# The end of attention and the gating of a fused attention and expert kernel: an own order for the last turn, a PSUM pool per bank, ten warm-up products instead of fourteen, and other queues for three loads of v and eighteen clears

## The chip, the cores and the metric

The kernel runs on one core of one Trainium2 chip. The time is device microseconds of one execution, as the median of the runs shown. The engines are TensorE (PE, with its weight loads as PEld), VectorE (DVE), ScalarE (ACT), GpSimd (POOL) and SyncE (SP). A queue of SP, ACT or POOL issues transfers to 16 DMA engines.

## The reference

Attention over 8 batches, 8 heads, 576 positions and 64 columns, with a causal mask over blocks of 64, then a layer of 8 experts in which each token goes to its best expert and an expert keeps its 80 tokens of the highest gate:

```python
scores = scale * np.matmul(q, k.transpose(0, 1, 3, 2))
scores = np.where(block_i >= block_j, scores, -1000000000.0)
attn = np.exp(scores - np.max(scores, axis=-1, keepdims=True))
attn = attn / (np.sum(attn, axis=-1, keepdims=True) + 1e-09)
x = np.matmul(attn, v)            # then (8, 8, 576, 64) -> (4608, 512)
logits = x @ w_gate
expert_idx = np.argmax(logits, axis=1)
probs = np.exp(logits - logits.max(-1, keepdims=True))
probs /= probs.sum(-1, keepdims=True) + 1e-09
gate_w = probs[np.arange(N), expert_idx]
for e in range(E):
    tok_idx = np.where(expert_idx == e)[0]
    if len(tok_idx) > capacity:
        tok_idx = tok_idx[np.argpartition(-gate_w[tok_idx], capacity)[:capacity]]
    h = np.maximum(x[tok_idx] @ w1[e], 0.0)
    out[tok_idx] = gate_w[tok_idx, None] * (h @ w2[e])
```

All tokens that no expert keeps have zeros in `out`, so at most 640 of 4608 rows carry a result and the rest must be cleared.

## The kernel before, in words

**Attention** goes by pairs of heads, 32 of them (4 in each of 8 batches, `NP = 4`). The program runs a loop over turns `i`, and in each turn a table `TURN` of (offset, operation) says what is issued for which pair: the loads five turns ahead, the transposes of q and k (DVE, L430) two turns ahead, the scores (PE, L459), the maxima (DVE, L476) and the exponentials (ACT, L487) of the pair after, and for the pair of the turn the transposes of the exponentials back (`back`, PE, L514, in four pieces A, B, C, L), the copies of these out of PSUM (`take`, ACT or DVE, L545, to `PT`), and the products with v (`values`, PE, L534). Two more copies, V0 and V1, put the result into `xT`; `flip` (DVE, L296) transposes it into `Y`, and `store` (SP, L300 to L303) writes `Y` and the reciprocal sums `rs` of a batch to `xs` in DRAM. PSUM has 8 banks, and a table gives each use its banks.

**Gating** comes once per batch of four pairs and is dealt out over later turns by the slots `pe`, `t` and `ta` of the table: `logits` (PE, L311, 8 products of 288 columns in two banks), two copies to `lgT` (ACT, L315), `logits2` (PE, L322, ten transposes), then on DVE `products` (L328), `shift`, `first_of` and `weight`, with `expo` on ACT between them, `turn` (L368, `sp`, on POOL for batches 0 to 6 and on DVE for batch 7), `turn2` (PE, L377) and `placed` (DVE, L383, to `Wt`). In the drain behind the last turn the rest of batch 6 goes first, then the whole chain of batch 7.

**The choice of tokens** follows: maxima of `Wt` (DVE, L705), `near` and `spread` (L714, L717), a ranking on PE (`ranked`, L727, into two PSUM tiles), counts on DVE and ACT (L772, L775), one-hot rows (L780), picks on PE (L788), and the list `gi` (L792). With it POOL issues eight gathers of 80 rows of `xs` (L802).

**The experts**: `divide` (DVE, L896) makes `xn` of gathered rows, `prepare` (L916) transposes it, `first` (PE, L907) and `second` (PE, L957) are the two products, and POOL scatters the results (L966). The weights are 16 matrices of 2 MB; three are loaded on POOL during attention, the others on SP (L256): one behind the last store of `xs`, two that wait for the first gather, and three that wait for the fourth.

**Warm-up products** (`warm`, L555) are matmuls of 128x512 whose result nothing reads. `WARM` gives their number for five places: 8 at the start of the program, 14 behind `logits2` of the last batch, 5 behind its `turn2`, 2 behind `ranked`, 12 behind the picks. The statement stands late in the program; `issue_after` names the instruction behind which the scheduler may put them.

**The queues**: `load_v` (L423, L425) issues three transfers per pair on POOL. `clear` (L163) writes 512 KB of zeros to `out`; 18 of them are needed. Nine are issued on POOL, one every third turn from turn 6, and the other nine on SP behind the stores of the last batch.

## Time and profile before

| what | value |
|---|---|
| median of three runs | 435.67 us (434.53 to 435.85) |
| the profiled execution | 436.88 us |
| its span, first to last instruction | 435.1 us |
| mean granted clock of TensorE | 0.95 |
| PE busy, share of the span | 389.9 us, 90% |
| ACT busy | 302.5 us, 70% |
| DVE busy | 276.1 us, 63% |
| POOL busy | 143.8 us, 33% |
| DMA moved | 84.31 MB, 194 GB/s over the span |

The profiled execution took 1.21 us more than the median of the runs, and its span is 1.78 us shorter than its own time. Attention fills the span up to about 298 us, the last gating and the choice of tokens the time up to about 322, and the experts the rest. A granted clock of 1.0 is 2.4 GHz, one of 0.5 is 1.2 GHz. A window's five engines are PE, PEld, DVE, ACT and POOL. In the rows of a timeline the first two numbers are the start and the length of a group of instructions in us; what stands in brackets is the idle time of the engine before it and the work that ended it.

### The profile page before, as it was taken

What the parts mean: (1) busy time and instruction counts of PE and PEld (TensorE: products, weight loads), DVE (VectorE), ACT (ScalarE), POOL (GpSimd) and SP (SyncE); (2) the same over time, 40 slices, a digit from 0 to 9 for tenths busy, and PEclk for the clock granted to TensorE, in tenths of its full rate; (3) what the DMA queues carried; (4) which work ended last, traced back from release to release, by engine and by line L of the source; (5) the groups of instructions that cost most, each with busy time, mean ns of one, the idle gap of its engine ahead of it and who ended that gap; (6) DMA issues with size and microseconds to landing.
All of it is one profiled execution on the core that took longest, in us unless ns stands there. A gap on an engine that the chain in (4) does not pass through costs nothing. (4 is left out here: it accounts for less than half of the span.)

```text
span 435.1 us, 13902 instructions
## 1 busy us (share of the span) xinstructions
PE 389.9 (90%) x5363; PEld 260.8 (60%) x5363; DVE 276.1 (63%) x768; ACT 302.5 (70%) x954; POOL 143.8 (33%) x273
## 2 busy tenths in 40 slices
PE   3799999999999999999999999985773999999960
PEld 2476666666766676676667666663553955555530
DVE  3568878998899799899898899873432130100010
ACT  0579999999999999999999999992020223333240
POOL 8523533454345335434454244200235001000010
PEclk9889999999999999999999999999666899999995
DMA  9999999899999999999899983140899999999000
GB/s 132 156 133 166 135 180 199 201 160 179 183 235 181 158 207 140 188 202 193 133 201 201 146 191 87 50 112 8 275 369 268 391 395 399 396 396 346 23 19 19
DMA packets 196071, 84.31 MB, mean 194 GB/s; under 512 B 160221, under 2 KB 178653, under 8 KB 196000
## 3 DMA queue, kind: packets, MB, share of 16 engines
q1 hardware_dynamic: 185424, 60.18, 64.0%
q0 software_dynamic: 8208, 22.89, 20.1%
q8 instruction: 44, 0.72, 0.8%
q10 hardware_dynamic: 2368, 0.30, 0.6%
q14 instruction: 27, 0.22, 0.2%
HBM read 63.21 MB, written 20.33 MB: 192 GB/s over the span
## 5 line engine op out<-in xcount | busy, mean ns | idle before, releaser
L487 ACT ACTIVATE P<-bank,negm 128x192 f32<-128x192 f32 (+2 forms) x320 | 162.2, 591 | 0.0
L459 PE MATMUL bank<-T,qt 64*128 64x320 f32 (+3 forms) x512 | 109.3, 516 | 7.8 <-POOL qt L437 4.1
L476 DVE TENSOR_REDUCE negm<-bank 128x1 f32<-128x192 f32 (+1 forms) x192 | 87.7, 472 | 27.2 <-PE bank L466 27.0
L545 ACT COPY PT<-bank 128x512 f32<-128x512 f32 x192 | 91.3, 584 | 8.3 <-PE bank L514 8.3
L534 PE MATMUL bank<-PT,vn 128*64 128x384 f32 (+5 forms) x768 | 93.8, 384 | 0.5 <-ACT PT L545 0.5
L487 ACT ACTIVATION_READ_ACCUMULATOR P<-bank,negm 128x1 f32 x320 | 89.6, 281 | 0.0
L514 PEld LDWEIGHTS bank<-ident,P 64*128 64x128 f32 x1664 | 66.0, 140 | 20.8 <-ACT PT L545 19.9
L437 POOL TENSOR_SCALAR qt<-T 128x512 f32<-128x512 f32 x64 | 28.0, 448 | 145.8 <-DVE raw L476 142.3
L514 PE MATMUL bank<-ident,P 64*128 64x64 f32 x1664 | 72.7, 227 | 1.3 <-ACT PT L545 0.7
L534 PEld LDWEIGHTS bank<-PT,vn 128*64 128x64 f32 x768 | 47.4, 137 | 40.6 <-issue 31.6
L459 PEld LDWEIGHTS bank<-T,qt 64*128 64x128 f32 x512 | 44.7, 191 | 23.1 <-issue 7.2
L423 POOL DMA_DIRECT2D vn<-in_v_dram x64 | 50.2, 786 | 0.3 <-issue 0.3
L476 DVE TENSOR_REDUCE raw<-bank 128x1 f32<-128x64 f32 (+1 forms) x128 | 48.5, 434 | 1.2 <-PE bank L459 1.2
L430 DVE STREAM_TRANSPOSE T<-ld 128x576 f32<-128x576 f32 x64 | 49.0, 767 | 0.2
L907 PEld LDWEIGHTS ps<-xsT,w 128*64 128x64 f32 x1024 | 38.5, 144 | 3.2 <-issue 1.9
L907 PE MATMUL ps<-xsT,w 128*64 128x80 f32 x1024 | 40.2, 241 | 0.0
L957 PE MATMUL av<-w,hT 128*32 128x512 f32 (+1 forms) x280 | 37.5, 594 | 0.0
L961 DVE SCALAR_TENSOR_TENSOR y<-av,comb,yt 80x512 f32<-80x512 f32 x7 | 5.2, 746 | 50.6 <-ACT yt L960 50.6
L966 POOL DMA_INDIRECT out_dram<-y,si x8 | 7.4, 924 | 82.3 <-DVE y L961 57.8
L456 PEld LDWEIGHTS bank<-T,qt 64*128 64x128 f32 x256 | 24.3, 196 | 12.0 <-issue 11.3
L957 PE MATMUL ps<-w,hT 128*32 128x512 f32 (+1 forms) x72 | 29.2, 548 | 0.0
L927 ACT ACTIVATE hT<-ps 128x320 f32<-128x320 f32 x16 | 7.0, 438 | 31.4 <-PE ps L907 31.4
(172 smaller groups left out, 399.0 us busy)
## 6 DMA issues: line engine op xcount, KB each, us to landing
w<-in_moe_w_dram SPq DMA_DIRECT2D x13, 2048.0 KB, 21.2
ld<-in_q_dram SPq DMA_DIRECT2D x128, 72.0 KB, 4.3
xs<-Y SPq DMA_DIRECT2D x32, 288.0 KB, 5.7
ld<-in_k_dram SPq DMA_DIRECT2D x124, 72.0 KB, 4.7
vn<-in_v_dram POOLq DMA_DIRECT2D x64, 128.0 KB, 4.4
out_dram<-zero POOLq DMA_DIRECT2D x9, 512.0 KB, 5.1
out_dram<-zero SPq DMA_DIRECT2D x9, 512.0 KB, 5.6
w<-in_moe_w_dram POOLq DMA_DIRECT2D x8, 512.0 KB, 6.7
```

Of the source, the lines that this page charges most:

```text
L423: nc.gpsimd.dma_start(self.vn[:, h], v[b, h0 + h, 0:512].rearrange("(j p) d -> p j d", p=P))
L430: nc.vector.transpose(t, self.nat[x].rearrange("p g d -> p (g d)"))
L437: nc.gpsimd.tensor_scalar(to, from_, scalar1=SCALE, scalar2=1.0, op0=ALU.mult, op1=ALU.mult)
L456: nc.tensor.matmul(s[h][:, c:c + n], lhsT=q_[:, b0:b0 + P], rhs=k_[:, k0:k0 + n], start=False, stop=False)
L459: nc.tensor.matmul(s[h][:, c:c + n], lhsT=q_[:, BLK + P * t:BLK + P * (t + 1)], rhs=k_[:, 0:n], start=(c == 0), stop=(g == "1"))
L476: nc.vector.tensor_reduce(to[:, b, h:h + 1], self.s[g][h][:, c:c + n], axis=AX.X, op=ALU.max, negate=True)
L487: nc.scalar.activation(Pt[self.i % 2][u][:, h, 0:n], self.s[g][h][:, c:c + n], AF.Exp, bias=self.negm[:, t, h:h + 1], scale=1.0, accum_out ...
L514: nc.tensor.transpose(pt[c][:, n_ * BLK:(n_ + 1) * BLK], row[u][r, h, P * j:P * (j + 1)], ident[r, r])
L534: nc.tensor.matmul(to, lhsT=self.vt[:, h, :] if j == 4 else self.vn[:, h, j, :], rhs=self.PT[:, h, row, b0:b1].rearrange("p b r -> p (b r) ...
L545: (nc.scalar.copy if TAKE[x] == "a" else nc.vector.tensor_copy)(*self.out.pop(x))
L907: yield nc.tensor.matmul(dst(b)[64 * c:64 * (c + 1)], lhsT=w_[:, a, col:col + 64], rhs=x_[:, a], start=(a == 0), stop=(a == n - 1))
L957: last = nc.tensor.matmul(to[col:col + s1 - s0, c0:c1], lhsT=hT[:, a, s0:s1], rhs=w_[:, a, c0:c1], start=(a == ends[0]), stop=(a == ends[1 ...
```

## The change

1. The last turn has a table of its own, `LAST`, with its own banks (`LAST_BANKS`): the pieces B, A, C and L go to banks 4 and 5, 0 and 1, 6 and 7, and 2, and `values` to bank 3. The copies of the pieces are split between ACT and DVE by name.
2. The loop ends with turn 31 and not two turns later. What followed in the two empty turns and the drain is written out: V0 of the last pair is copied half by ACT and half by DVE, the logits of the last batch are issued ahead of the last two flips, the second copy to `lgT` goes to DVE, `turn2` of batch 6 comes behind `logits2` of batch 7 in bank 3, and `turn2` of batch 7 goes to bank 2.
3. PSUM has one pool per bank instead of one pool with eight tiles, and behind attention the pool `ps_m2` is made second instead of last, so that the uses behind attention fall on other banks.
4. Fourteen warm-up products behind `logits2` become ten, behind `turn2` of batch 6.
5. `load_v` of pairs 0, 1 and 2 goes to SP.
6. The eighteen clears are all on POOL: four at the start of each of the turns 27 to 30, and two at the start of turn 31.

```diff
-WARM = [8, 14, 5, 2, 12]
+WARM = [8, 10, 5, 2, 12]
...
+LAST_BANKS = {"B": (4, 5), "A": (0, 1), "C": (6, 7), "L": (2,), "av": (3,)}
+LAST = (
+    (0, "pe"),
+    (0, "back", "B"),
+    (-1, "take", "V1", "v"),
+    (0, "soft", "34", 1),
+    (-1, "take", "V0", "v"),
+    (0, "back", "A"),
+    (0, "take", "B0", "v"),
+    (0, "take", "B1", "a"),
+    (0, "t"),
...
+    (0, "back", "C"),
+    (0, "take", "A1", "a"),
+    (0, "take", "A0", "v"),
+    (0, "back", "L"),
+    (0, "take", "C0", "a"),
+    (0, "take", "C1", "v"),
+    (0, "take", "L", "a"),
+    (0, "values"),
+    (0, "t"),
...
+    (0, "ta"),
+    (0, "t"),
...
-    psp = attp.enter_context(tc.tile_pool(name="psp", bufs=1, space=PSUM))
+    psp = [attp.enter_context(tc.tile_pool(name=f"psp{i}", bufs=1, space=PSUM)) for i in range(8)]
...
+        def logits_out(self, lt):
             for c in range(2):
-                nc.scalar.copy(lgT[:, BLK + 288 * c:BLK + 288 * (c + 1)], lt[c][:, 0:288])
+                copy = nc.vector.tensor_copy if c and self.b == B - 1 else nc.scalar.copy
+                copy(lgT[:, BLK + 288 * c:BLK + 288 * (c + 1)], lt[c][:, 0:288])
...
         def load_v(self):
+            eng = nc.sync if self.i < 3 else nc.gpsimd
...
-        for i in range(-LEAD, n + 2):
+        for i in range(-LEAD, n):
...
-            if i >= 4 and i % 3 == 0 and i < n:
+            for _ in range(4 if i >= n - 5 else 0):
                 clear(cleared)
                 cleared += 1
...
-        while pe_ or small or acts:
-            pe()
-            for _ in range(8):
-                t()
-            ta()
-            if turns:
-                bt, mark = turns.pop(0)
-                bt.turn2(banks("g")[0])
-                mark()
         bt = batches[B - 1]
         for _ in bt.recip():
             pass
+        to, from_ = pairs[n - 1].out.pop("V0")
+        half = to.shape[1] // 2
+        pairs[n - 1].take("V1", "v")
+        nc.scalar.copy(to[:, 0:half], from_[:, 0:half])
+        nc.vector.tensor_copy(to[:, half:], from_[:, half:])
+        lt = bt.logits_of()
+        for p_ in pairs[n - 2:]:
+            p_.flip()
         bt.store()
-        bt.logits()
+        bt.logits_out(lt)
+        ta()
+        while not turns:
+            t()
         bt.logits2()
+        bt_, mark = turns.pop(0)
+        bt_.turn2(banks("av")[0])
+        mark()
         for _ in (*bt.products(), *bt.shift()):
             pass
         bt.expo()
+        while small:
+            t()
         for _ in (*bt.first_of(), *bt.weight()):
             pass
         bt.turn(nc.vector, 2)
-        bt.turn2(banks("g")[0])
+        bt.turn2(banks("L")[0])
...
     ps_s = ctx.enter_context(tc.tile_pool(name="ps_s", bufs=2, **ps))
+    ps_m = ctx.enter_context(tc.tile_pool(name="ps_m2", bufs=3, **ps))
     ps_s4 = ctx.enter_context(tc.tile_pool(name="ps_s4", bufs=1, **ps))
     ps_a = ctx.enter_context(tc.tile_pool(name="ps_a", bufs=1, **ps))
-    ps_m = ctx.enter_context(tc.tile_pool(name="ps_m2", bufs=3, **ps))
...
-    for k, ins in enumerate((bt.turned, bt.last, ranked, picked)):
+    for k, ins in enumerate((bt_.last, bt.last, ranked, picked)):
         warm(WARM[1 + k], wt[:, k % 2], ins)
```

On PE, from the end of attention to the ranking, the kernel before has this order; `bank` with `sp` is `turn2`, `bank` with `xT` the logits, `bank` with `lgT` the ten transposes of `logits2`, and `ps` with `identr` the warm-up products:

```order
L377 MATMUL bank_5528<-sp,sameR_110 32x40 [waits Pool_49]
L311 MATMUL bank_5549<-xT,wgd 32x288 [waits DVE_49]
...
L322 MATMUL bank_5561<-ident,lgT 128x64 [waits Activation_49]
...
L377 MATMUL bank_5596<-sp,sameR_110 32x40 [waits DVE_49,PE_49]
...
L555 MATMUL ps_5774<-identr 128x512 x19
L727 MATMUL ps<-spread,before_117 128x96 [waits DVE_49,PE_49]
```

And the changed kernel this one:

```order
L345 MATMUL bank_5555<-xT,wgd 32x288 [waits DVE_49]
...
L360 MATMUL bank_5581<-ident,lgT 128x64 [waits Activation_49]
L360 MATMUL bank_5582<-ident,lgT 128x64 [waits DVE_49]
...
L415 MATMUL bank_5593<-sp,sameR_110 32x40 [waits Pool_49]
L415 MATMUL bank_5593<-sp,sameR_110 32x40 x7
L595 MATMUL ps_5801<-identr 128x512 x10
L415 MATMUL bank_5626<-sp,sameR_110 32x40 [waits DVE_49]
...
L595 MATMUL ps_5801<-identr 128x512 x5
L774 MATMUL ps<-spread,before_117 128x96 [waits DVE_49,PE_49]
```

`turn2` of batch 6 has moved from ahead of the logits to behind `logits2`; before, all nineteen warm-up products stand behind `turn2` of batch 7 and ahead of the ranking, and now ten of them stand ahead of that `turn2` and five behind it.

On SP, behind the stores of the last batch, the kernel before has these rows, `zero` being the clears and `w` the weights of the experts:

```order
L303 DMA xs<-Y 32x18x128 x4
L163 DMA out_dram<-zero 128x1024 x9
L256 DMA w<-in_moe_w_dram 128x4x1024
L256 DMA w<-in_moe_w_dram 128x8x512
L256 DMA w<-in_moe_w_dram 128x4x1024
L256 DMA w<-in_moe_w_dram 128x8x512
```

And the changed kernel these:

```order
L335 DMA xs<-Y 32x18x128 x4
L288 DMA w<-in_moe_w_dram 128x4x1024
L288 DMA w<-in_moe_w_dram 128x8x512
L288 DMA w<-in_moe_w_dram 128x4x1024 x2
L288 DMA w<-in_moe_w_dram 128x8x512
```

The nine clears are gone from between the last store and the first of these weights, and two weights of the kind 128x4x1024 (`w1`) now follow each other, the second of them ahead of a `w2`.

On POOL, at the start of the program, the kernel before issues v of pair 0 between the clearing of `wgd` and the first constants:

```order
L569 MEMSET wgd 128x128
L423 DMA vn<-in_v_dram 128x4x64 x2
L425 DMA vt_139<-in_v_dram 64x2x64
L198 MEMSET dl 128x45
L199 MEMSET zero 128x1024
```

In the changed kernel the constants follow at once:

```order
L609 MEMSET wgd 128x128
L230 MEMSET dl 128x45
L231 MEMSET zero 128x1024
```

Three issues of transfers have left POOL ahead of its constants.

## Rows read from the trace of the kernel before

**Rows 1.** Windows: from:to, length, busy us (instructions) of five engines, clock, DMA share, GB/s.

```profile
270.00:280.00 10.00, 9.97 (x140) 6.57 (x136) 9.13 (x24) 10.00 (x38) 3.44 (x7) 1.00 0.22 81
300.00:310.00 10.00, 5.13 (x63) 3.43 (x64) 6.52 (x31) 1.03 (x3) 1.23 (x4) 0.62 0.49 109
360.00:370.00 10.00, 10.00 (x180) 5.90 (x176) 0.75 (x1) 2.92 (x5) 0.92 (x1) 1.00 1.03 400
19.00:26.00 7.00, 6.31 (x64) 5.49 (x66) 3.00 (x7) 4.73 (x19) 0.00 (x0) 0.51 1.03 134
```

**Rows 2.** Timeline of the start: issues on ACT and POOL, first work of DVE.

```profile
0.78 2.12 ACTq L415 DMA_DIRECT2D ld<-in_k_dram  x4
3.03 1.78 POOL L423 DMA_DIRECT2D vn<-in_v_dram  x2
4.76 0.67 POOL L425 DMA_DIRECT2D vt<-in_v_dram  x1
...
9.20 0.17 DVE L226 TENSOR_TENSOR iota_c<-sameR,iota_c 128x16 f32<-128x16 f32 x1 [1.69 <-POOL iota_c L224]
...
9.59 1.44 DVE L430 STREAM_TRANSPOSE T<-ld 128x576 f32<-128x576 f32 x2
```

**Rows 3.** DMA issues of 1.2 to 2.5 us: count, KB each, us to landing.

```profile
ld<-in_k_dram ACTq DMA_DIRECT2D x4, 72.0 KB, 4.0
```

**Rows 4.** Timeline of the last turn and the last gating.

```profile
291.03 1.97 PE L514 MATMUL bank<-ident,P 64*128 64x64 f32 x48 [0.57 <-DVE prod L328]
...
294.70 2.70 PE L534 MATMUL bank<-PT,vn 128*64 128x384 f32 x20 [0.52 <-ACT PT L545]
...
299.67 0.79 POOL L368 TENSOR_TENSOR sp<-Gm,sameE 128x320 f32<-128x320 f32 x1 [21.77 <-DVE Gm L360]
...
301.21 1.18 PE L311 MATMUL bank<-xT,wgd 128*32 128x288 f32 x16 [0.35 <-DVE Wt L383]
...
303.69 0.68 DVE L328 TENSOR_TENSOR prod<-bank,rs 128x80 f32<-128x80 f32 x4 [1.51 <-PE bank L322]
```

**Rows 5.** Timeline of the ranking: warm-up products and what stands around them.

```profile
307.55 0.50 PE L377 MATMUL bank<-sp,sameR 128*32 128x40 f32 x16 [3.80 <-DVE sp L368]
307.99 6.77 PE L555 MATMUL ps<-identr 128*128 128x512 f32 x19
...
309.22 0.61 DVE L717 TENSOR_TENSOR spread<-near,sameR 128x192 f32<-128x192 f32 x2
...
314.60 0.58 PE L727 MATMUL ps<-spread,before 128*128 128x96 f32 x4
```

**Rows 6.** Timeline from the clears on SP to the first expert.

```profile
307.37 11.72 SPq L163 DMA_DIRECT2D out_dram<-zero  x9
...
321.76 1.11 POOL L802 DMA_INDIRECT xg<-xs,gi  x1 [9.21 <-ACT occ L849]
...
331.41 0.81 DVE L896 TENSOR_TENSOR xn<-xg 80x256 f32<-80x256 f32 x2 [10.53 <-DMA xg<-xs,gi]
```

**Rows 7.** DMA issues, whole program, then of 319 to 320, then of 416 to 424.

```profile
xg<-xs,gi POOLq DMA_INDIRECT x8, 9.9
...
w<-in_moe_w_dram SPq DMA_DIRECT2D x1, 2048.0 KB, 16.9
...
out_dram<-y,si POOLq DMA_INDIRECT x2, 2.9
```

**Rows 8.** Timeline of PE in the first two experts.

```profile
334.92 7.05 PE L907 MATMUL ps<-xsT,w 128*64 128x80 f32 x128
...
342.32 4.65 PE L907 MATMUL ps<-xsT,w 128*64 128x80 f32 x128
```

**Rows 9.** The clears on POOL: ns min/median/max, first and last start, us to landing.

```profile
L163 POOL DMA_DIRECT2D out_dram<-zero x9: 584/584/612, 71.0 to 277.0; - x9
...
DMA to landing us min/median/max: 4.6/5.3/6.4
```

**Rows 10.** Timeline of POOL in one turn late in attention.

```profile
267.94 0.88 POOL L437 TENSOR_SCALAR qt<-T 128x512 f32<-128x512 f32 x2 [4.98 <-DVE raw L476]
```

More of the change, by code (lines that the diff above doesn't have):

```diff
@@ L91 @@
     (3, "load_v"),
+)
+LAST_BANKS = {"B": (4, 5), "A": (0, 1), "C": (6, 7), "L": (2,), "av": (3,)}
[11 more added lines that the diff above has]
+    (0, "t"),
+    (0, "t"),
+    (0, "back", "C"),
[6 more added lines that the diff above has]
+    (0, "values"),
+    (0, "t"),
+    (0, "t"),
+    (0, "t"),
+    (0, "t"),
+    (0, "ta"),
+    (0, "t"),
+    (0, "t"),
+    (0, "t"),
 )
@@ L271, in tile_attn_moe, with banks @@
     attp = ExitStack()
-    psp = attp.enter_context(tc.tile_pool(name="psp", bufs=1, space=PSUM))
-    def banks(use):
-        return [psp.tile([P, 512], F32, name=f"bank{i}") for i in BANKS[use]]
+    psp = [attp.enter_context(tc.tile_pool(name=f"psp{i}", bufs=1, space=PSUM)) for i in range(8)]
+    def banks(use, where=BANKS):
+        return [psp[i].tile([P, 512], F32, name=f"bank{i}") for i in where[use]]
     class Batch:
@@ L306, in logits, with logits_of @@
         def logits(self):
+            self.logits_out(self.logits_of())
+        def logits_of(self):
             lt = banks("g")
@@ L313, in logits @@
                                      tile_position=(0, 32 * pr))
+            return lt
+        def logits_out(self, lt):
             for c in range(2):
-                nc.scalar.copy(lgT[:, BLK + 288 * c:BLK + 288 * (c + 1)], lt[c][:, 0:288])
+                copy = nc.vector.tensor_copy if c and self.b == B - 1 else nc.scalar.copy
+                copy(lgT[:, BLK + 288 * c:BLK + 288 * (c + 1)], lt[c][:, 0:288])
         def logits2(self):
@@ L403, in __init__ @@
             self.out = {}
+            self.where = LAST_BANKS if i == n - 1 else BANKS
             self.T = {}
@@ L420, in load_v @@
             b, h0 = self.b, self.h0
+            eng = nc.sync if self.i < 3 else nc.gpsimd
             self.vn = ld.tile([P, 2, 4, D], F32, name="vn", bufs=4)
             for h in range(2):
-                nc.gpsimd.dma_start(self.vn[:, h], v[b, h0 + h, 0:512].rearrange("(j p) d -> p j d", p=P))
+                eng.dma_start(self.vn[:, h], v[b, h0 + h, 0:512].rearrange("(j p) d -> p j d", p=P))
             self.vt = VT[self.i % 4]
-            nc.gpsimd.dma_start(self.vt[0:BLK], v[b, h0:h0 + 2, 512:576].rearrange("h p d -> p h d"))
+            eng.dma_start(self.vt[0:BLK], v[b, h0:h0 + 2, 512:576].rearrange("h p d -> p h d"))
         def prep(self, x):
@@ L498, in back @@
                 self.PT = big.tile([P, 2, 4, 8, BLK], F32, name="PT")
-            pt = banks(x)
+            pt = banks(x, self.where)
             halves = [slice(c * BLK, (c + 1) * BLK) for c in range(2)]
@@ L522, in values @@
         def values(self):
-            (av,), a0 = banks("av"), self.last[:, 4 * BLK:5 * BLK]
+            (av,), a0 = banks("av", self.where), self.last[:, 4 * BLK:5 * BLK]
             if turns:
@@ L541, in flip, with take @@
             self.bt.flip(self.pr)
-        def take(self, x):
-            (nc.scalar.copy if TAKE[x] == "a" else nc.vector.tensor_copy)(*self.out.pop(x))
+        def take(self, x, eng=None):
+            (nc.scalar.copy if (eng or TAKE[x]) == "a" else nc.vector.tensor_copy)(*self.out.pop(x))
     def warm(n, wt, after=None):
@@ L633, in tile_attn_moe @@
                 next(early, None)
-            for d, what, *args in TURN:
+            for d, what, *args in TURN if i < n - 1 else LAST:
                 if what in slots_:
                     slots_[what]()
-                elif 0 <= i + d < n and not (what == "flip" and i + d >= n - NP):
+                elif 0 <= i + d < n and not (what == "flip" and n - NP <= i + d < n - 2):
                     getattr(pairs[i + d], what)(*args)
-            if n - NP <= i + valued < n:
+            if n - NP <= i + valued < n - 2:
                 pairs[i + valued].flip()
```

## The prediction, before the run

> **What bounds the kernel now.** I read the windows first, since each stage has its own limit. Late in attention ACT is busy for 10.00 of 10 us and PE for 9.97: nothing but less work or an earlier start helps there. In the experts PE is busy for 10.00 of 10 while the weights arrive at 400 GB/s. Between the two, from 300 to 310, PE has work for 5.13 us, DVE for 6.52, ACT for 1.03 and POOL for 1.23 [rows 1]: a chain of single steps, and every microsecond taken out of it is a microsecond of the end. So I then read the timeline of that chain [rows 4 to 6], and the start, where the first work is a chain too [rows 2, 3]. A measurement of this kernel can tell about 0.3% (1.3 us) from no change.
>
> **Part 1, v of three pairs on SP.** DVE's first transpose T starts at 9.59, right behind the product with iota_c at 9.20, which waited for POOL. POOL's constants wait in line behind three issues for v, from 3.03 to 5.43 [rows 2]. Without these 2.4 us the constants end 2.4 us earlier and T could start at 7.2. Its data are there: k of pair 0 is issued on ACT from 0.78 to 2.90, and lands 4.0 later, at 6.9 [rows 2, 3]. I take a gain of **2.3**; the bounds are 0 (q or k lands just before 9.59) and 2.4. On SP the nine issues stand behind the loads of pairs 2, 3 and 4. What they push back there is pair 3 and later, wanted a turn (8.25 us, the distance of POOL's two issues for successive pairs) or more after the start: no cost, and if that cover fails, nine issues of about 0.53 (k: 2.12 for four) are 4.8 us on SP, of which the spare turn takes all.
>
> **Part 2, the last turn and the last gating.** Before, the 48 transposes at 291.03 waited 0.57 for DVE's `prod` in banks that they share, and `values` came at 294.70. With banks of its own the last turn has no such wait; with V0 moved from ACT, which copies the pieces, to DVE, I take 0.6, so `values` runs from 294.1 to 296.8 and, with half a copy of V0 on each engine and two flips of some 0.8, DVE is done at 299.3. The logits don't wait for the flips, and their second copy goes to DVE: the ten transposes can follow at 299.75, and DVE's products at 300.5. Before, the rest of batch 6 stood in between: its `sp` on POOL at 299.67, then turn2 and placed, so that the logits began at 301.21 and the products at 303.69 [rows 4]. That is 3.2 earlier. What is late next is batch 6 itself: its `sp` still comes at about 300.4 to 301.2, but now only its own turn2 waits for it.
>
> **Part 3, the warm-up products and the ranking.** `spread` was done at 309.83, yet the ranking started at 314.60: PE was running nineteen warm-up products from 307.99 to 314.76 (6.77, 0.356 each) [rows 5]. These 4.8 us lay on the path. Now ten of them run behind turn2 of batch 6, from about 301.6: 3.6 us, to 305.2. From products to `spread` is 309.83 - 303.69 = 6.14, and turn2 of batch 7 comes 3.86 into it, at 307.55 [rows 5]. So turn2 could start at 304.35 and has to wait to 305.2, 0.85 more; behind it `spread` takes 2.28 to 307.5, which the five remaining products (1.8) just fit. The ranking starts at 307.7 instead of 314.6: **6.9**, part 2 included. Bounds: no wait, 7.8. At the clock of 0.62 in that window [rows 1] a product took 0.356, so at 0.5 it takes 0.44, the ten end at 306.0 and the wait is 1.7; with the flips 0.3 late the low end is 5.8.
>
> **Part 4, pools.** One pool per bank lets a use wait for its own bank only: in no row but the 0.57 of part 2 does it matter. In the new order of the ranking the tile that ACT counts from is finished one group later: I take 0.3 off, between 0 and 0.45 (a group of 0.58 overlaps the next). **-0.3.**
>
> **Part 5, the clears.** Nine clears on SP took 11.72 us to issue from 307.37, ahead of a weight of 2 MB that landed 16.9 after its issue at 319.5. So the first gather, at 321.76, met a full set of queues: its `xn` came at 331.41, 9.65 later [rows 6, 7]; the eight gathers' median is 9.9, and the last two scatters, of the same size of rows in empty queues, took 2.9 [rows 7]. Now the stores end near 303.6, only that one weight follows (at 400 GB/s [rows 1] 5.2 us, with the stores ahead of it some 8: landed near 312), and the gather comes at about 315. From both sides: 2.9 as in empty queues, 9.65 as now. Being issued into queues that are empty but for its seven followers it is nearer the 2.9; I take 4.5, a gain of **5.15** (0 to 6.75). The Trainium skill, "DMA: Bandwidth & Descriptors", section "Anatomy of one DMA — SWDGE (gpsimd) path", gives about 2.0 us and the bytes over 436 GB/s for a transfer that GpSimd issues: an estimate of 2.4 us for 80 rows of 2080 bytes, by which the sum would be 2.1 us less, 417.5.
>
> Their new place costs nothing as long as POOL has room: it waits 4.98 of each turn for DVE [rows 10], four issues of 0.584 to 0.612 [rows 9] need 2.4, and the DMA share from 270 to 280 is 0.22 [rows 1], as no loads of q and k are left. The cover ends at 4.98/4 = 1.25 per issue; the nearest dearer row is SP's, 11.72/9 = 1.30, by which five turns would lose 0.2 each, 1 us. Before, the nine issues on POOL fell into turns in which DVE was busy (9.13 of 10 in 270 to 280), and the longest took 0.612. The Trainium skill, "SBUF — State Buffer", section "A bandwidth-pool intuition that's wrong (but worth ruling out)", says that a transfer issued by GpSimd that takes some 620 ns alone takes some 3100 beside a VectorE copy; four of those would need 12.4 us a turn, 7.4 more than is free, and the sum would be some 33 us worse. The trace disagrees so far, with 0.612 as its longest; I give that rule 1 chance in 100, among those of slower.
>
> **Part 6, the first expert.** From the first `xn` at 331.41 to the full row of the second expert at 342.32 are 10.9 us. In them 128 products take 7.05, which take 4.65 in the row behind [rows 8]: PE came out of its wait for the gather at the lower clock. With that wait shorter (twelve warm-up products, 4.3 us, nearly fill 4.5) most of the 2.4 comes back. I take **2.0**; bounds 0 (the low clock stays) and 3.2 (2.4, and the second divide of 0.81 [rows 6], which the first products no longer stand behind). The fourth `w1` now goes ahead of a `w2` on SP and waits for the first expert's products to end: that `w2` then lands some 7 us ahead of its use. No cost, and no gain, since PE is full from there on [rows 1].
>
> **Sum.** 2.3 + 6.9 - 0.3 + 5.15 + 2.0 = 16.05. The profiled execution would go from 436.88 to 420.8; it stands 1.21 above the median, so the median goes from 435.67 to **419.6**. All bounds at their best give 20.15 (415.5), all at their worst 5.35 (430.3).
>
> **Rivals.**
> - *The gathers stay slow* (15%). If what fills the queues at 322 is the weights and not the clears, 9.65 stays and part 5 gives 0: 424.8. For it: the weight landed 16.9 after its issue, so it flowed right through the gathers. Against: it waited behind 4.7 MB of clears.
> - *The start is held by loads* (10%). If q of pair 0 lands only at 9.5, part 1 gives nothing: 421.9.
> - *The start gains more* (8%). From 19 to 26 the clock is 0.51 and PE has 6.31 busy us of 7 [rows 1]. If the earlier v or the shifted constants close the idle time ahead of it, half of 6.31 comes back, 3.1: 416.5.
> - *POOL's queue blocks* (4%, slower). In the order of POOL each transfer waits for the one eight places back. With three loads of v and four clears a turn, that one was issued 8/7 of a turn before, 9.4 us. A clear lands 4.6 to 6.4 after its issue [rows 9]: nothing waits. But if the landing stretches to the 16.9 of the weight [rows 7], each turn becomes 16.9 x 7/8 = 14.8 instead of 8.25, and qt of the next pair, behind the clears on POOL, is that late: four turns of 6.5, 26 us, 445.7. It decides at a landing of 9.4; for it speaks only that clears will now follow each other at 0.6, against it the DMA share of 0.22.
> - *Nothing shows* (1%): part 2 and 3 are given back whole in a later wait, and the gathers too.
>
> **How the numbers follow.** The forecast as summed has 61%, the named rivals the rest, and 1% is for other mishaps. The first three rivals and the bounds of the forecast's own terms lie between 414 and 426, where I leave out the all-worst sum and the slower case: that holds some 8 in 10. Faster by over 0.3%: 0.95; within: 0.01; slower: 0.04.
>
> **What would show it.** T on DVE near 7.2; products of batch 7 some 3 us earlier against the end of the last `soft` and the ranking right behind `spread`, with ten warm-up products ending by 306 less the start's gain; clears on POOL of 0.6, with POOL's qt no later in its turn; SP's weight right behind the stores; the first `xg` landing in under 6 us; the first expert's 128 products at under 6 us. The forecast is wrong if turns 27 to 31 are longer than 8.25, if the landing of the clears exceeds 9.4, or if `xn` still waits 9 us behind the first gather.

## The result, and the profile of the changed kernel

The changed kernel takes **420.6 us** (median of four runs, 419.72 to 421.09) against 435.76 of the kernel before on the same chip (434.53 to 436.12): a ratio of **0.9656**, with a 95% interval of 0.9637 to 0.9674. The profiled execution took 421.09, with a span of 419.3. The profiled execution before had a span of 435.1, so 15.8 us are to be found. Some executions of a kernel come out several per cent longer than its others, and the ratios leave these out. Line numbers of the changed kernel are 32 to 47 higher (`ranked` is L774, `first` L954, `second` L1004, the gathers L849).

The table follows the same places through both timelines. "Gained here" is the growth of the lead since the row above.

| place | before | after | lead | gained here |
|---|---|---|---|---|
| first transpose T on DVE | 9.59 | 7.20 | 2.39 | 2.39 |
| first product with v | 28.07 | 24.04 | 4.03 | 1.64 |
| `values` of the last turn | 294.70 | 289.55 | 5.15 | 1.12 |
| `products` of batch 7 on DVE | 303.69 | 295.47 | 8.22 | 3.07 |
| ranking begins on PE | 314.60 | 302.81 | 11.79 | 3.57 |
| first gather | 321.76 | 310.24 | 11.52 | -0.27 |
| first `xn` | 331.41 | 313.38 | 18.03 | 6.51 |
| first product of `second` | 351.71 | 336.15 | 15.56 | **-2.47** |
| last scatter | 423.13 | 407.31 | 15.82 | 0.26 |

The start, in the timeline of DVE and PE; these rows answer to [rows 2]:

```profile
6.81 0.18 DVE L258 TENSOR_TENSOR iota_c<-sameR,iota_c 128x16 f32<-128x16 f32 x1 [1.68 <-POOL iota_c L256]
...
7.20 1.44 DVE L470 STREAM_TRANSPOSE T<-ld 128x576 f32<-128x576 f32 x2
...
8.78 1.02 PE L499 MATMUL bank<-T,qt 64*128 64x448 f32 x4 [1.05 <-POOL qt L477]
```

T again follows the product with iota_c and never waits for its data. The first four products of scores take 1.02 us; before, PE had idled for 4.13 ahead of them, and the same four took 1.86. That row and those behind it give 1.2 of the 1.64.

The last gating and the ranking, in the timeline ([rows 4, 5]):

```profile
289.55 2.70 PE L574 MATMUL bank<-PT,vn 128*64 128x384 f32 x20 [0.92 <-ACT PT L585]
...
292.87 1.18 PE L345 MATMUL bank<-xT,wgd 128*32 128x288 f32 x16 [0.39 <-DVE xT L585]
...
295.47 0.69 DVE L366 TENSOR_TENSOR prod<-bank,rs 128x80 f32<-128x80 f32 x4
295.65 0.79 POOL L406 TENSOR_TENSOR sp<-Gm,sameE 128x320 f32<-128x320 f32 x1 [19.16 <-PE bank L360]
...
296.78 4.07 PE L595 MATMUL ps<-identr 128*128 128x512 f32 x10
...
298.99 0.56 DVE L406 TENSOR_TENSOR sp<-Gm,sameE 128x160 f32<-128x160 f32 x2
300.77 0.37 PE L415 MATMUL bank<-sp,sameR 128*32 128x40 f32 x16
301.08 1.43 PE L595 MATMUL ps<-identr 128*128 128x512 f32 x5
...
302.32 0.61 DVE L764 TENSOR_TENSOR spread<-near,sameR 128x192 f32<-128x192 f32 x2
...
302.81 0.66 PE L774 MATMUL ps<-spread,before 128*128 128x96 f32 x4 [0.30 <-DVE spread L764]
```

From `values` to `products` there are 5.92 us instead of 8.99, as batch 6's `sp` no longer stands in between. The ten warm-up products take 4.07 and hold the last turn2 to 300.77, though its `sp` was done at 299.55: 1.2 us given back. But the ranking now follows `spread` at once.

The gathers and the first experts, in the timeline of POOL, DVE and PE ([rows 6, 8]):

```profile
310.24 1.12 POOL L849 DMA_INDIRECT xg<-xs,gi  x1 [4.61 <-DMA w<-in_moe_w_dram]
313.38 0.76 DVE L943 TENSOR_TENSOR xn<-xg 80x256 f32<-80x256 f32 x2 [4.04 <-DMA xg<-xs,gi]
...
315.35 0.91 PE L954 MATMUL ps<-xsT,w 128*64 128x80 f32 x18 [0.51 <-ACT xsT L964]
...
316.61 4.36 PE L954 MATMUL ps<-xsT,w 128*64 128x80 f32 x119
322.87 0.91 PE L954 MATMUL ps<-xsT,w 128*64 128x80 f32 x19 [1.89 <-issue]
...
324.13 3.68 PE L954 MATMUL ps<-xsT,w 128*64 128x80 f32 x100
...
330.16 0.44 PE L881 MATMUL ps<-RG,OH 128*80 128x24 bf16 x7 [2.06 <-issue]
...
330.88 3.89 PE L954 MATMUL ps<-xsT,w 128*64 128x80 f32 x62
...
334.82 1.40 PE L954 MATMUL ps<-xsT,w 128*64 128x80 f32 x32
```

The first gather is used 3.14 us after its issue, against 9.65. The Trainium skill's fit for a transfer that GpSimd issues ("DMA: Bandwidth & Descriptors", section "Anatomy of one DMA — SWDGE (gpsimd) path") gave an estimate of 2.4; the trace is nearer to it than to the 4.5 that I took. The first expert's products run at full pace (119 in 4.36; before, 128 in 7.05). Then PE stops twice, for 1.89 and 2.06 us, for nothing that the profile shows ("issue"), and 62 products take 3.89 us that take 2.43 in `e13_shift`, for one.

The mark `second` does not stand behind the same work in both kernels. Before, 128, 128 and these two groups of products stood ahead of it, 322 in all:

```profile
348.42 1.60 PE L907 MATMUL ps<-xsT,w 128*64 128x80 f32 x38
...
350.59 1.19 PE L907 MATMUL ps<-xsT,w 128*64 128x80 f32 x28
```

In the changed kernel the six groups above make 350. At 36.6 ns each (119 in 4.36) the 28 more, of the third expert, are 1.0 us of work done earlier and not lost. From the first `xn` to the end of product 322 there are 20.4 us before and 21.9 after: for the same work the loss is 1.5 and not 2.47.

The clears on POOL, by line, answer to [rows 9]:

```profile
L195 POOL DMA_DIRECT2D out_dram<-zero x18: 532/536/598, 250.1 to 275.7; - x18
its engine sat idle before it (us, times) until:
  DMA out_dram<-zero: 0.7, 2
...
DMA to landing us min/median/max: 4.9/7.1/11.5
```

They cost what they cost before, and two of them waited 0.7 us together for an older transfer. The starts of successive products with v, up to those of turn 30, stand 8.25 to 9.36 us apart late in attention in both timelines, so the turns keep their length; 8.25 was never the length of each of them.

### The profile page after: what moved, and what is told of

Read it like the earlier page. It is cut to its first block, busy times and chain, and to the rows that moved or that the text cites. A ratio compares the mean times of both kernels' runs of the same rounds, so it can differ in the third digit from the quotient of the medians.

```text
span 419.3 us, 13895 instructions
## 1 busy us (share of the span) xinstructions
PE 384.6 (92%) x5359; PEld 256.4 (61%) x5359; DVE 279.6 (67%) x773; ACT 300.4 (72%) x950; POOL 141.7 (34%) x273
## 3 DMA queue, kind: packets, MB, share of 16 engines
q0 software_dynamic: 9120, 26.72, 21.7%
## 5 line engine op out<-in xcount | busy, mean ns | idle before, releaser
L499 PE MATMUL bank<-T,qt 64*128 64x320 f32 (+3 forms) x512 | 107.1, 507 | 5.7 <-ACT P L527 3.9
L585 ACT COPY PT<-bank 128x512 f32<-128x512 f32 (+1 forms) x190 | 90.3, 586 | 8.0 <-PE bank L554 8.0
L499 PEld LDWEIGHTS bank<-T,qt 64*128 64x128 f32 x512 | 43.6, 187 | 20.4 <-issue 7.4
L463 POOL DMA_DIRECT2D vn<-in_v_dram x58 | 45.8, 792 | 1.0 <-PE bank L506 0.7
L954 PE MATMUL ps<-xsT,w 128*64 128x80 f32 x1024 | 40.2, 238 | 2.4 <-issue 1.9
L954 PEld LDWEIGHTS ps<-xsT,w 128*64 128x64 f32 x1024 | 38.0, 141 | 5.9 <-issue 4.6
L1004 PE MATMUL av<-w,hT 128*32 128x512 f32 (+1 forms) x280 | 37.5, 594 | 0.0
L1007 ACT ACTIVATE yt<-ps,gfar 32x512 f32<-32x512 f32 (+1 forms) x18 | 11.4, 635 | 28.5 <-PE ps L1004 28.4
L496 PEld LDWEIGHTS bank<-T,qt 64*128 64x128 f32 x256 | 23.7, 191 | 11.6 <-issue 10.8
L1004 PE MATMUL ps<-w,hT 128*32 128x512 f32 (+1 forms) x72 | 29.1, 547 | 0.0
```

What stands on the lines that cost most here:

```text
L463: eng.dma_start(self.vn[:, h], v[b, h0 + h, 0:512].rearrange("(j p) d -> p j d", p=P))
L496: nc.tensor.matmul(s[h][:, c:c + n], lhsT=q_[:, b0:b0 + P], rhs=k_[:, k0:k0 + n], start=False, stop=False)
L499: nc.tensor.matmul(s[h][:, c:c + n], lhsT=q_[:, BLK + P * t:BLK + P * (t + 1)], rhs=k_[:, 0:n], start=(c == 0), stop=(g == "1"))
L585: (nc.scalar.copy if (eng or TAKE[x]) == "a" else nc.vector.tensor_copy)(*self.out.pop(x))
L954: yield nc.tensor.matmul(dst(b)[64 * c:64 * (c + 1)], lhsT=w_[:, a, col:col + 64], rhs=x_[:, a], start=(a == 0), stop=(a == n - 1))
L1004: last = nc.tensor.matmul(to[col:col + s1 - s0, c0:c1], lhsT=hT[:, a, s0:s1], rhs=w_[:, a, c0:c1], start=(a == ends[0]), stop=(a == ends[1 ...
```

## The experiments

Each edit is made to the changed kernel. The change's own runs stand at 420.6 and 0.9656; a ratio is to the kernel before, run beside the edited one.

**v of three pairs back on POOL** (`e1_v_pool`).

```diff
-            eng = nc.sync if self.i < 3 else nc.gpsimd
+            eng = nc.gpsimd
```

> The changed kernel with the three loads of v back on POOL. Theory A, the start is one chain through POOL's constants, and PE, which then idles 4.1 us ahead of its first scores, runs these at half pace (1.86 us for four against 1.02): the first transpose on DVE goes from 7.2 back to 9.6, the first product with v from 24.0 back to 28.1, and the time from 420.6 to 424.6. Theory B, only the 2.4 us of the transpose hang on it and the rest of the 4.0 came from the clears or the pools: 423.0. Theory C, the loads of q and k would hold the start anyway: 420.6.

Measured: 420.13 us, ratio 0.9639 (0.96 to 0.9677): the time of theory C, by another way. The start goes back as theory A says (T at 9.59, first product with v at 27.31, 0.8 short of its 28.1), and the last scatter comes at 410.72 instead of 407.31, 3.4 later. But behind it there are 7.4 us to the end instead of 12.0. Of these 4.6 us 3.8 are one instruction of POOL, the long one of its three drains at the end; the other 0.8 lie ahead of it (its start stands 6.1 behind the last scatter in the changed kernel and 5.3 here). Here is the line that holds it (min/median/max in ns), of the changed kernel and then of this run:

```profile
L1224 POOLq DRAIN  x3: 46/114/4977, 413.4 to 419.0; - x3
```

```profile
L1224 POOLq DRAIN  x3: 46/114/1220, 416.0 to 417.8; - x3
```

So part 1 is worth 3.4 us up to the last scatter, and the edit changes the drain as well. Before the change the long drain took 4.81: it has no share in the 15.8.

**The clears back in their old places** (`e2_clears`).

```diff
-            for _ in range(4 if i >= n - 5 else 0):
+            for _ in range(1 if i >= 4 and i % 3 == 0 else 0):
```

> The changed kernel with the clears back in their old places (nine on POOL every third turn, nine on SP behind the last stores). Theory A, the clears fill the queues that the gathers meet: from the first gather to its first use 9 to 10 us instead of 3.1, so 6.5 later there; behind it PE should get back the two pauses of 1.9 and 2.1 us that it has in the changed kernel, so the time is 423.0 to 427.1. Theory B, the weights fill the queues: 3.1 stays and the time is 420.6.

Measured: 424.88, ratio 0.9756 (0.9711 to 0.98), in theory A's range. The first gather is issued at 310.05 and used at 316.64: 6.6 us instead of 3.1, less than the 9 to 10 that I expected. From the first product of the first expert to its `second` there are 17.6 us (321.51 to 339.14) instead of 20.8, but 1.0 of this is the order (322 products stand ahead of `second` again). And the first of them comes 4.9 us behind the first `xn` instead of 2.0, so that from `xn` to `second` only 0.3 comes back of what the gathers lose (22.5 us against 22.8). The last scatter is 3.9 later; the long drain is shorter by 1.1 (3.83).

One thing of the old place is not back. Before the change SP issued the next weight 2.3 us ahead of the first gather (321.76); here it does so 0.4 behind it (310.05). The two lines, of the kernel before and of this run:

```profile
319.47 25.98 SPq L256 DMA_DIRECT2D w<-in_moe_w_dram  x5
```

```profile
310.41 16.56 SPq L288 DMA_DIRECT2D w<-in_moe_w_dram  x4
```

**Six warm-up products instead of ten** (`e6_warm6`).

```diff
-WARM = [8, 10, 5, 2, 12]
+WARM = [8, 6, 5, 2, 12]
```

> Six warm-up products behind turn2 of batch 6 instead of ten. Theory A, the last turn2 waits for them (1.3 us by the trace): the ranking and the gather come 1.3 earlier and the time is 419.3. Theory B, the microsecond is lost again behind the gather, where PE waits for nothing that the profile shows: gather 1.3 earlier, time 420.6. Theory C, a lower clock eats it: gather at the same place, 420.6 or more.

Measured: 421.67 (419.14 to 423.14), ratio 0.9662 (0.9605 to 0.9718): theory C, with the gather 0.7 later. In PE's timeline the last turn2 is 1.2 us earlier, and everything behind it slower:

```profile
299.57 0.60 PE L415 MATMUL bank<-sp,sameR 128*32 128x40 f32 x16 [0.55 <-DVE sp L406]
300.10 2.50 PE L595 MATMUL ps<-identr 128*128 128x512 f32 x5
302.40 1.00 PE L774 MATMUL ps<-spread,before 128*128 128x96 f32 x4
```

From 300 to 305 the granted clock is 0.51 here, the lower level, after an idle time of 0.55 on PE; in the changed kernel it is 1.00 from 301 to 305, and the same rows take 0.37, 1.43 and 0.66. The 1.2 us that the ten products hold up turn2 buy the clock of the ranking.

**Five weights held until the last gather** (`e7_hold`).

```diff
-    HOLD = 3
+    HOLD = 7
...
-    weights(FWA - 1, fetches[0])
+    weights(FWA - 1, fetches[HOLD])
```

> The five weights that wait for the first or the fourth gather wait for the eighth, so the queues stay open some 8 us longer. Theory A, PE's two pauses of 1.9 and 2.1 us in the first experts are waits for its own instructions, whose loads stand in queues full of weights: the first pause goes, the gathers land sooner than their median of 8.1, and the time is 416.6 to 418.6. Theory B, the pauses are waits for weights: they grow, and the time is 423 or more. Theory C, the pauses have to do with neither: 420.6.

Measured: 430.7, ratio 0.9881 (0.9841 to 0.9922). The windows of the first expert refute theory A:

```profile
316.00:318.00 2.00, 1.04 (x24) 0.90 (x20) 0.64 (x7) 0.27 (x1) 1.70 (x2) 1.00 0.49 121
318.00:320.00 2.00, 0.64 (x5) 0.43 (x4) 0.49 (x2) 0.16 (x1) 1.60 (x4) 0.78 0.43 129
```

The queues are less than half busy (0.49 and 0.43), and PE has work for 1.68 of 4 us all the same; from the first product to `second` there are 21.7 us. The ten microseconds are lost late: two starts of `second` stand 18.0 apart (374.19 and 392.21) where the widest distance of the changed kernel is 12.0, and all that the edit moved is the weights; which of them is late was not followed. So B is right in its time, but not about the pauses: the way to `second` did not grow by more than 1 us.

**One PSUM pool for the eight banks** (`e4_one_pool`).

```diff
-    psp = [attp.enter_context(tc.tile_pool(name=f"psp{i}", bufs=1, space=PSUM)) for i in range(8)]
+    psp = [attp.enter_context(tc.tile_pool(name="psp", bufs=1, space=PSUM))] * 8
```

> The changed kernel with one PSUM pool for the eight banks, as before. By the order of PE all fifteen warm-up products then stand behind the last turn2 and none ahead of it. Theory A, the pool per bank is what lets ten of them run ahead of the last turn2, and their place is worth what the ranking gained by it: turn2 comes 1.3 us earlier, at 299.5, but the ranking waits for fifteen products, some 5 us, to 304.9 instead of 302.8: 2 us more, 422.6. Theory B, pools matter for nothing but waits on banks in the last turn: less than 0.6 us, 420.6 to 421.2.

Measured: 424.84, ratio 0.9738 (0.97 to 0.9777), 4.2 us more: theory A, and twice its size. PE's timeline:

```profile
299.73 0.60 PE L415 MATMUL bank<-sp,sameR 128*32 128x40 f32 x16 [2.51 <-DVE sp L406]
300.68 5.77 PE L595 MATMUL ps<-identr 128*128 128x512 f32 x15 [0.35 <-DVE Wt L421]
306.29 0.58 PE L774 MATMUL ps<-spread,before 128*128 128x96 f32 x4
```

All fifteen products wait until the last use of the pool is over (`Wt` on DVE) and then stand ahead of the ranking, which is 3.5 later.

**The table of all turns for the last turn** (`e5_turn`, and the same kernel again as `e5b_turn`).

```diff
-            for d, what, *args in TURN if i < n - 1 else LAST:
+            for d, what, *args in TURN:
...
-            self.where = LAST_BANKS if i == n - 1 else BANKS
+            self.where = BANKS
...
         while not turns:
+            pe()
             t()
+            ta()
```

> The changed kernel with the table of all turns, and its banks, for the last turn too; the drain stays as it is now. Theory A, the table LAST gives what the first product with v gained in the last turn, 1.1 us of the 5.15 by the trace: values 1.1 later, and since the rest of batch 6's gating then follows the turn, up to 1 us more: 421.7 to 422.7. Theory B, the drain alone gave the gain of the gating: 420.6.

Measured: 424.99, ratio 0.9747 (0.9717 to 0.9777), outside both theories. The profiled execution took 430.67 us, 5.7 more than this median, so the kernel was run again:

> The same kernel as the run with the table of all turns in the last turn, whose profile shows a turn of 15 us that its other executions can't have had. Theory A, by its undisturbed parts the table LAST is worth 1.1 us up to the values and 0.9 from there to the ranking: 422.6. Theory B, there is a third loss in the turns ahead, and the time is 424 to 425 again.

Measured: 424.76, ratio 0.9735 (0.9687 to 0.9782). Time: theory B; cause: neither. From `values` of turn 30 to that of turn 31 there are 7.62 us instead of 6.49 (1.13), from there to the ranking 13.92 instead of 13.26 (0.66). The turns ahead are 0.45 later, as in `e7_hold` and `e13_shift`. The third loss is behind the gather, where PE's order, which the scheduler makes, changed with it:

```profile
316.30 0.49 PE L965 MATMUL pm<-ident,xn 80*128 80x80 f32 x4 [0.74 <-DVE xn L945]
318.07 0.50 PE L965 MATMUL pm<-ident,xn 80*128 80x80 f32 x4 [1.28 <-DVE xn L945]
```

The second expert's transposes stand ahead of the first expert's products here, which begin 2.2 us behind the first transposes instead of 1.1.

**The first product with 128 weight columns** (`e10_first128`).

```diff
             for a in range(n):
-                for c in range(2):
-                    col = (2 * b + c) * 64
-                    yield nc.tensor.matmul(dst(b)[64 * c:64 * (c + 1)], lhsT=w_[:, a, col:col + 64], rhs=x_[:, a],
-                                           start=(a == 0), stop=(a == n - 1))
+                yield nc.tensor.matmul(dst(b), lhsT=w_[:, a, b * P:(b + 1) * P], rhs=x_[:, a],
+                                       start=(a == 0), stop=(a == n - 1))
```

> The first product of each expert is issued as 32 products with 128 weight columns instead of 64 with 64: the same sums, half the instructions. Theory A, PE waits for its own instructions in the first experts: the pauses without a releaser (1.9 and 2.1 us, and the slow third row) go, and from the first product of the first expert to the second product of it there are 17 us or less instead of 20.8: up to 4 less, 416.6 to 419. Theory B, the pauses have another cause (data that the profile doesn't tie to PE): they stay, and the time is 420.6, or more if 128 columns run slower on PE than twice 64.

Measured: 435.15, 436.68, 454.85 and 456.09 us. In the profile, of the execution of 436.68, the pauses are gone, but a product takes 114 ns (62 in 7.09 us) where two of 64 columns take 73 (119 in 4.36), so PE may never get far enough ahead to be held up: inconclusive for the cause.

**Nine transfers more on POOL** (`e11_tail`), and **three loads of v issued twice** (`e12_dup`).

```diff
-            eng.dma_start(self.vt[0:BLK], v[b, h0:h0 + 2, 512:576].rearrange("h p d -> p h d"))
+            if 10 <= self.i < 19:
+                for h in range(2):
+                    eng.dma_start(self.vt[0:BLK, h], v[b, h0 + h, 512:576])
+            else:
+                eng.dma_start(self.vt[0:BLK], v[b, h0:h0 + 2, 512:576].rearrange("h p d -> p h d"))
```

> Nine of POOL's loads of the tail of v are issued in two halves, so POOL issues nine transfers more, as many as in the run with v of three pairs back on POOL; nothing else changes. In that run the time from the last scatter to the end was 7.4 us instead of 12.0, POOL's last drain 1.2 instead of 5.0. Theory A, the drain's length follows the number of transfers that POOL has issued: 7.4 again, time 416.0. Theory B, it follows something else of that run (its later start, the order on POOL): 12.0 stays, 420.6.

Measured: 420.91, ratio 0.9642 (0.9607 to 0.9677); the long drain takes 4.977: theory B. At the start, which the edit does not touch (T at 7.19), this execution has the four products of scores at their pace from before the change:

```profile
8.78 1.87 PE L503 MATMUL bank<-T,qt 64*128 64x448 f32 x4 [0.80 <-POOL qt L481]
```

```diff
-                eng.dma_start(self.vn[:, h], v[b, h0 + h, 0:512].rearrange("(j p) d -> p j d", p=P))
+                for _ in range(2 if 10 <= self.i < 13 else 1):
+                    eng.dma_start(self.vn[:, h], v[b, h0 + h, 0:512].rearrange("(j p) d -> p j d", p=P))
...
-            eng.dma_start(self.vt[0:BLK], v[b, h0:h0 + 2, 512:576].rearrange("h p d -> p h d"))
+            for _ in range(2 if 10 <= self.i < 13 else 1):
+                eng.dma_start(self.vt[0:BLK], v[b, h0:h0 + 2, 512:576].rearrange("h p d -> p h d"))
```

> The changed kernel, in which POOL issues the loads of v of pairs 10, 11 and 12 twice (the same data): as many rows of transfers more as the run with v of three pairs on POOL had, while the start keeps its gain. Theory A, the length of POOL's last drain follows the rows that POOL has described, not the number of transfers: 1.2 us instead of 5.0, 7.4 from the last scatter to the end instead of 12.0, time 416.5. Theory B, the drain has to do with something else: 12.0 stays, 420.6.

Measured: 439.6, ratio 1.0066 (1.0032 to 1.0099), and yet theory A holds for what it was about: the long drain takes 1.220, and 7.4 us lie behind the last scatter. The time was lost elsewhere, by my edit: the second load of a tile waits for the first, so POOL waited six times, 22.2 us together, with the next pair's `qt` behind it.

**48 more instructions for PE** (`e13_shift`).

```diff
+        if k == 3:
+            with tc.issue_after(ranked.ins):
+                for i in range(24):
+                    nc.tensor.matmul(wt[:, 0, 0:16], lhsT=ones, rhs=ones[:, 0:16], start=(i == 0), stop=(i == 23))
```

> 24 small products (48 instructions of PE), which nothing reads, stand behind the two warm-up products of the ranking, where PE is idle for 2.7 us. Theory A, PE waits for its own instructions in the first experts: what it has in stock is used up 24 products sooner, the first pause comes that much earlier (20 to 28 products into the first expert instead of 44 to 137), and the way from the first product of the first expert to its second product changes by 0.5 us or more from 20.6. Theory B, the pauses hang on data: they stay in their place, 20.6 stays, time 420.6.

Measured: 423.03, ratio 0.9688 (0.9642 to 0.9734). The pauses begin after 44 products, as in the runs with six warm-up products (43) and with v on POOL (44), and not 24 sooner. By their place theory B. The way to `second` is 22.1 instead of 20.8, which B did not give, but `e11_tail`, whose edit lies elsewhere, has 21.5, so 22.1 is hardly clear of the spread. The place tells against a plain stock of instructions.

**The last five gathers behind the first expert, and six loads of k on POOL** (`e15_gathers`).

```diff
-    for e in range(E):
+    def gather(e):
...
+    for e in range(3):
+        gather(e)
...
-    HOLD = 3
+    HOLD = 2
...
             finish(divided)
+            for g in range(3, E):
+                tc.add_manual_dep(gather(g).ins, done[1].ins.name, mybir.DependencyInfo(
+                    mybir.DependencyClass.Sync, mybir.DependencyReason.DATA))
...
-                        (nc.scalar if x == 1 and self.i == 0 else nc.sync).dma_start(
+                        (nc.scalar if x == 1 and self.i == 0 else
+                         nc.gpsimd if x == 1 and (self.i == 20 or self.i == 22 and h == 0) else nc.sync).dma_start(
```

> Two edits to the changed kernel, read in two places of the trace. First, POOL issues the last five gathers only when the first expert's first products are done (the weights that waited for the fourth gather wait for the third). In all runs so far PE's pauses in the first expert end 1 to 3 us behind the issue of the last gather, and in the kernel before, whose gathers were all issued when that expert began, there was none. Theory A, the pauses come with the issuing of gathers: the first expert's 128 products take 5.6 us or less without a pause, and from the first product of the first expert to its second product there are 17 to 18 us instead of 20.6: 3 us less. Theory B, they come with PE's own instructions or with the weights: 20.6 or more, since the late gathers meet full queues. Second, six loads of k (pairs 20 and 22) are issued on POOL instead of SP, 3456 rows as in the run with v on POOL. Theory A, the drain follows the rows that POOL describes: 1.2 us, 7.4 from the last scatter to the end. Theory B, it follows bytes or something else: 12.0. With A and A the time is 414, with A in the drain alone 416.8, with neither 420.6 or more.

Measured: **417.77**, ratio **0.957** (0.9541 to 0.9598), the fastest of all. PE's timeline:

```profile
315.77 0.91 PE L959 MATMUL ps<-xsT,w 128*64 128x80 f32 x18 [0.52 <-ACT xsT L969]
...
317.04 4.36 PE L959 MATMUL ps<-xsT,w 128*64 128x80 f32 x119
323.23 0.91 PE L959 MATMUL ps<-xsT,w 128*64 128x80 f32 x19 [1.83 <-issue]
...
324.49 5.32 PE L959 MATMUL ps<-xsT,w 128*64 128x80 f32 x100
...
332.26 1.33 PE L959 MATMUL ps<-xsT,w 128*64 128x80 f32 x32
333.52 0.62 PE L1009 MATMUL av<-w,hT 128*32 128x512 f32 x3
```

To `second` there are 17.75 us instead of 20.8, with 334 products ahead of it instead of 350; for the same 322 products there are 17.4 instead of 19.9. The second pause is gone and the first (1.83) stayed. The slow row is not gone: 100 products take 5.32 here, which take 3.68 in the changed kernel, while the next 46 are back at full pace (1.88). So of theory A's two signs the time to `second` came and the stretch without a pause did not. The gain is lost again in the later experts, where PE waits 3.8 us in all instead of 1.1 (from 333 and from 336 to 405): the last scatter comes at 408.34, 1.0 later than in the changed kernel. Which of the edit's moves costs that was not tried. The long drain takes 1.62 instead of 4.98, between the 1.2 of theory A and the 5.0 of B, and that is what the kernel gains: its span is 416.5.

## Why the prediction was right, and where it was not

The forecast was 419.6 and the time is 420.6, but this is the sum of four terms that were 4.0 too small together and of one that was 4.5 too large. That the total came so near is luck. The terms are read from one profiled execution of each kernel.

- **Part 1** (2.3): 4.03 at the first product with v. The chain through POOL's constants is right to a tenth (2.39), and q and k were there: the rival of late loads falls. The rest, 1.64, has half the size of the rival of a larger start (3.1). That it comes from PE's shorter idle time ahead of the scores is not shown: in `e11_tail` PE idles for 0.80 only, and yet the same four products take 1.87 and the first product with v comes at 25.68. In the ten other edited runs with T at 7.2 it stands between 23.8 and 25.5. So 2.39 is firm, and the size of the rest is not.
- **Part 2** (0.6 to `values`, 3.2 to `products`): 1.12 and 4.19. Shown by the table taken back: its banks and copies give 1.13, and without it there are still 6.67 us from `values` to `products` instead of 8.99, which leaves 2.3 of the 3.07 to what is written out behind the loop.
- **Part 3** (6.9 with part 2): 7.76, which is 11.79 less the start's 4.03. The warm-up products held turn2 for 1.2 where I took 0.85, at 0.407 each.
- **Part 4** (-0.3): -0.27 for the order of the ranking. But "in no row but the 0.57 of part 2 does it matter" was wrong, though it did not touch the sum: with one pool all fifteen products stand ahead of the ranking, and the kernel is 4.2 slower. The order excerpts showed the ten ahead of turn2; I did not ask what let them stand there.
- **Part 5** (5.15): 6.51, near its bound of 6.75. Taking the clears back costs 4.3 in time and 3.45 at the gather, so they make up about half of the 6.51. The other 3.06 is open, and the rival that the weights fill the queues is not refuted for it: before, the next weight was issued 2.3 ahead of the first gather, with the clears back 0.4 behind it, and in the changed kernel it had landed (at 310.11). The landing of the clears passed 9.4 (11.5 at most), which the prediction names as a sign that it is wrong and as the point from which the slower rival decides. It cost POOL 0.7 us, with `qt` still waiting for DVE: the point was right as a bound, but two late landings are not eighteen. The rule of the Trainium skill ("SBUF — State Buffer", section "A bandwidth-pool intuition that's wrong (but worth ruling out)") that spoke against POOL did not show: 0.598 us is the longest of eighteen, while DVE was busy for 7.13 of 8 us (262 to 270).
- **Part 6** (2.0): -2.47 at `second`, -1.5 for the same work. In the stretch that it was about the term was too small: from the first `xn` to the second expert's products there were 10.9 us and are 7.1 (313.38 to 320.47), a gain of 3.8, beyond its bound of 3.2, and the pace came back as said (119 products in 4.36). The step that failed is "No cost, and no gain, since PE is full from there on": from there to `second` there are 15.7 us instead of 9.4. Two pauses make 3.95 of them (0.74 of idle time before), the slow row 1.5 and the 28 products 1.0. I had read "full" from the window of 360 to 370, and out of a kernel in which PE came late and slow to that stretch, and so never met what now holds it.

What holds PE there is not settled. It isn't weights in the queues (`e7_hold`), and the place of the pauses tells against a plain stock of instructions (`e13_shift`). Part of it seems to come with the gathers. For the same 322 products PE needs 18.8 to 20.7 us in the nine kernels, the changed one among them, that have these products and the gathers in their place, 17.4 with the last five moved away, and 16.9 and 17.7 in the two kernels whose first expert began when all eight gathers were issued (the kernel before and `e2_clears`). But `e2_clears` still has a pause of 1.4. And that the second pause went with the gathers is not shown, since it is missing in the other eight of the nine as well. These have three or four shorter stops instead, which begin after 43 to 47 products and are over 11.3 to 11.5 us behind the issue of the first gather, 1.1 to 1.4 behind the end of the last one's. The two pauses of the changed kernel end 12.6 and 19.9 behind the first, so what is expected for `e15_gathers`, that all pauses end 1 to 3 us behind the issue of the last gather, does not hold for them.

By what way a gather holds PE was not tried. The DMA view is a hint and no proof: in the changed kernel it lists loads of 16 KB of instructions from 320.17 to 321.42 and from 327.62 to 328.71, and both pauses begin within 0.9 us behind the start of one and end 1.45 behind its end; in `e15_gathers` the pause ends 1.49 behind such a load. But in `e13_shift` PE stops between 317.5 and 320.6 with the nearest of these loads at 308.7 and 327.4.

## What to carry to other kernels

Follow one list of places through both timelines, not the total: here the total was right and one of its terms had the wrong sign. Count the work ahead of each place, too: 28 products that had changed sides looked like a loss of 1.0 us. An engine that gets to a stretch earlier and faster than before meets limits there that the old trace can't show, so a stretch that "stays full" deserves a bound on both sides. And what a scheduler makes of a change (the place of warm-up products, the order of two experts' transposes) is worth a look in the order itself, since an edit far away moves it by a microsecond or more.

## What was not expected

The long drain of POOL stands at the end of every profile here, and it depends on what POOL's queue has carried. It took 4.81 us before and 4.977 after the change, and the same 4.977 in seven of the edited kernels, however late their end came. It took 3.83 with half of the clears on SP, and 1.22 in the two runs in which POOL described 3456 rows of v more (six loads of 128 x 4 and three of 64 x 2); nine transfers more with the same rows left it at 4.977, and as many shorter rows of k (six loads of 32 x 18) gave 1.62. So the number of transfers does not set it. That the rows do is not shown: 3456 more gave 1.22 and 1.62, and before the change, with the 3456 rows of v but nine clears fewer on POOL, it was 4.81. It is worth up to 3.8 us, as much as a part of this change.
